# One transfer instead of two for each of Q, K and V of a batch

## The chip, the cores and the metric

The kernel runs on one core of a Trainium2 chip. The metric is the device time of one execution in microseconds (us), less is better. The engines have short names: PE multiplies matrices (PEld is its weight load), DVE and ACT work on vectors, POOL and SP issue transfers here. Sixteen DMA engines move data between the chip's main memory and the core's on-chip memory, which has 128 partitions.

## What is computed

A sliding-window attention over 8 batches, 8 heads, 576 positions and 64 columns feeds a mixture of experts with 32 slots. Heads 0 to 3 are *plain*: a query sees the last 32 positions. Heads 4 to 7 are *dilated*: it sees every fourth of the last 128.

```python
batch, n_heads, seq, head_dim = (8, 8, 576, 64)

scores = scale * np.matmul(q, k.transpose(0, 1, 3, 2))
rel = pos[:, None] - pos[None, :]
mask_plain = (rel >= 0) & (rel < window)
mask_dil = (rel >= 0) & (rel < window * dilation) & (rel % dilation == 0)
masks = np.stack([mask_plain if h < H // 2 else mask_dil for h in range(H)], axis=0)
scores = np.where(masks[None, :, :, :], scores, -1000000000.0)
...
attn = np.exp(scores)
attn = attn / (np.sum(attn, axis=-1, keepdims=True) + 1e-09)
return np.matmul(attn, v).astype(np.float32)
```

The result, turned so that a row holds the 512 columns of one position (8 heads of 64), is the `x` (4608 x 512) of the second part:

```python
logits = x @ phi
d = np.exp(logits - logits.max(0, keepdims=True))
d /= d.sum(0, keepdims=True) + 1e-09
slot_input = (d.T @ x).reshape(E, S_per_e, D)
for e in range(E):
    h = np.maximum(slot_input[e] @ w1[e], 0.0)
    slot_out[e] = h @ w2[e]
c = np.exp(logits - logits.max(1, keepdims=True))
c /= c.sum(1, keepdims=True) + 1e-09
return (c @ slot_out).astype(np.float32)
```

There are 8 experts with 4 slots each; `w1[e]` is 512 x 1024 and `w2[e]` 1024 x 512. All inputs and the output are fp32.

## The kernel before

**Loads.** Every input is fp32 in main memory and is written as fp16 by the transfer itself. All these transfers are issued by POOL (`nc.gpsimd.dma_start`) and run in one queue, in the order of issue; only the constants come from SP. `load_raw(which, b)` brings Q, K or V of batch `b` into a tile of 128 partitions with `PJ * D` = 36 x 64 = 2,304 elements each. A head has 576 positions, that is `PB` = 16 pieces of 36 positions; a piece is one partition's row. Before, the loop over `g` at L188 issues two transfers of 64 rows each: `g = 0` the four plain heads into the even partitions (`t[0::2, :]`), `g = 1` the four dilated heads into the odd ones. Partition 2i holds row i of the plain heads, partition 2i + 1 row i of the dilated ones. Each tile name has two buffers (`bufs=2` of `raw_pool`, L161).

The experts' weights come by `load_w1` (L195, one transfer of 1 MB as written) and `load_w2` (L203, the whole of an expert in 1 MB, for experts 0 to 4; L209, in four transfers of 256 KB each, for experts 5 to 7).

**Turning.** DVE's `turn` (L220) transposes blocks of 32 x 32 words of a raw tile, all 128 partitions at once, in two halves along the row: `QT0`, `QT1` and so on. It puts Q and K into `qT` and `kT` and V into `vT`, in the tiles named `qk` and `vT` by the profile. Plain and dilated rows come out side by side, since their partitions alternate.

**The loop.** The list `ORDER` holds the steps of an iteration with a stage each; a step of stage s works on batch `it - s` (L529 to L537). After the later half of a turn has run, its raw tile is free and the load of the same tensor two batches on is issued (`frees`, `loads`). After V of batch 3 and of each later one a weight is issued too (`load_weights(1)`), and after V of batch 7 all that are left of w1 of the eight experts and w2 of experts 0 to 2. The remaining w2 take the place of the raw tiles and the `qk` tiles; they are issued when the last batch's turns and its scores `S2` are done (L538 to L549).

One iteration works on several batches: scores on PE (L262), exp on ACT (L271), masks on DVE (L282), the product with V on PE (L305), its normalisation (L317, L326, L330), the logits and the sums for the slots (`U`). After the loop PE multiplies the slots by w1 (L598) and w2 (L629), and the result is spread, multiplied by `ET` (L656), scaled (L665, L669) and written out batch by batch (L676, L703), also from POOL's queue.

**Before the loop** (L449 to L465) POOL issues in this order: Q and K of batch 0, V of batch 0, Q and K of batch 1, `phi`, V of batch 1.

Of the kernel before, what the change touches and what calls it, by code (L numbers as in the profile page):

```python
# [31 lines left out]
PJ = S // PB  # L32
# [64 lines left out]
def kernel(  # L97
# [10 lines left out]
    nc = tc.nc  # L108
# [75 lines left out]
    def load_raw(which, b):  # L184
        t = raw_pool.tile([128, PJ * D], FP16, name=f"raw{which}_{b}", tag=f"raw{which}")
        raw[(which, b)] = t
        src = {"Q": q, "K": k, "V": v}[which][b]
        for g in range(2):  # L188
            nc.gpsimd.dma_start(  # L189
                out=t[g::2, :],  # L190
                in_=src[4 * g : 4 * g + 4].rearrange("h (p j) d -> (h p) (j d)", j=PJ),
            )

    def load_w1(e):
        nc.gpsimd.dma_start(  # L195
# [253 lines left out]
    for which in "QK":  # L449
        load_raw(which, 0)  # L450
# [3 lines left out]
    for i in range(2):  # L454
        nc.vector.memset(vX[i][:, :, :, D : D + 1], 1.0)
        for x in (xp_t[i], xd_t[i]):
            nc.vector.memset(x[:, :, 4 * D : 4 * D + 1], 1.0)
    load_raw("V", 0)
    for which in "QK":
        load_raw(which, 1)  # L460
    nc.gpsimd.dma_start(
        out=phi_raw.rearrange("p (u c) s -> p u (c s)", u=2),
        in_=moe_phi.rearrange("(u p c) s -> p u (c s)", u=2, c=2),
# [65 lines left out]
    for it in range(B + max(s for _, s in STEPS)):  # L529
# [20 lines left out]
        if it == 0:  # L550
            nc.vector.tensor_copy(
                out=phi4, in_=phi_raw[:, :, None, :].broadcast_to([128, 4, 4, N_SLOTS])
# [54 lines left out]
    for c in range(8):  # L607
# [3 lines left out]
        out=hTm[:, 0].rearrange("p c (j s) -> p c j s", j=4)[:, :, :, 0:16], in_=hT4[:, :, :, 0:16]  # L611
    )
    nc.scalar.copy(
        out=hTm[:, 1].rearrange("p c (j s) -> p c j s", j=4)[:, :, :, 16:32], in_=hT4[:, :, :, 16:32]
# [87 lines left out]
    for e in range(2):  # L702
        nc.gpsimd.dma_start(  # L703
            out=rest[:, e, 512:576, :].rearrange("n i d -> i n d"), in_=om_l[64 * e : 64 * e + 64]
# [37 lines left out]
```

## Time and profile before

| what | us |
|---|---|
| time, median of 3 runs | 180.59 (180.25 to 180.80) |
| the profiled execution's own time | 180.63 |
| its span | 178.8 |
| busy: PE, DVE, ACT, POOL | 126.7, 126.3, 124.0, 56.2 |
| raw loads: transfers, KB written each, median from issue to landing | 16 each of Q, K and V, 288.0, 9.8 to 10.8 |
| 1 MB weights: transfers, median from issue to landing | 13, 22.1 |

How to read it: the span goes from the first to the last instruction or landing of one profiled execution. "Landing" is the moment when all sixteen DMA engines have signalled that their share of a transfer is written. A transfer waits behind the earlier ones of its queue, so the time from issue to landing is mostly waiting. The page gives the transfers of this execution:

```profile
DMA packets 21445, 40.85 MB, mean 229 GB/s; under 512 B 1712, under 2 KB 14128, under 8 KB 20784
q0 software_dynamic: 21280, 40.41, 114.3%
q1 hardware_dynamic: 144, 0.14, 0.3%
HBM read 62.07 MB, written 9.44 MB: 400 GB/s over the span
```

MB and GB/s in the first three lines count what is written, so an fp32 input counts half of what is read. A packet is one row or piece that a DMA engine moves in one go; the packets under 512 B include each engine's signal at the end of its share of a transfer. Shares over 100% come from packets that overlap on an engine. In lists of instructions a group of the same line is shown with its count (x2), and "L189" is line 189 of the kernel.

### The profile page before, as it was taken

How to read it: one execution, taken by the hardware profiler on the slowest of the kernel's cores; microseconds unless marked ns; L12 is line 12 of the kernel's file. 1: busy time of each engine (PE TensorE's matmuls, PEld its weight loads, DVE VectorE, ACT ScalarE, POOL GpSimd, SP SyncE). 2: the span in 40 equal slices, each digit the busy share in tenths (PEclk: the TensorE clock that was granted, in tenths of full speed). 3: DMA queues.
4: the chain of work that ended last, by engine and by line, in shares of the span. 5: the costliest groups of instructions: out<-in, count | busy, mean ns of one | idle time of the engine just before them, and what ended most of it. 6: DMA issues, size and time to landing. Idle time of an engine off the chain costs nothing.

```text
span 178.8 us, 4810 instructions
## 1 busy us (share of the span) xinstructions
PE 126.7 (71%) x2016; PEld 81.9 (46%) x2016; DVE 126.3 (71%) x277; ACT 124.0 (69%) x268; POOL 56.2 (31%) x94
## 2 busy tenths in 40 slices
PE   0015938988899998888988988986686856688000
PEld 0014625776666676567667657665332422221000
DVE  6464899999999999999999898275211016789200
ACT  6006758999999999999999989996301116688000
POOL 7544244224224224225420005111111515375400
PEclk9999999999999879999999699699957685555555
DMA  5999999999999999999999999999999999999994
GB/s 98 195 208 211 211 213 211 212 213 215 215 213 213 213 213 214 213 211 218 210 213 214 214 215 221 215 218 218 209 211 194 196 197 234 390 321 393 406 413 125
DMA packets 21445, 40.85 MB, mean 229 GB/s; under 512 B 1712, under 2 KB 14128, under 8 KB 20784
## 3 DMA queue, kind: packets, MB, share of 16 engines
q0 software_dynamic: 21280, 40.41, 114.3%
q8 instruction: 16, 0.26, 0.5%
q1 hardware_dynamic: 144, 0.14, 0.3%
q14 instruction: 5, 0.04, 0.1%
HBM read 62.07 MB, written 9.44 MB: 400 GB/s over the span
## 4 chain that ended last, share of the span: by engine, by line
DMA 56%; DVE 25%; PE 5%; issue 4%; ACT 3%; POOL 1%; POOLq 0%; DVEq 0%
DMA w<-in_moe_w_dram 36%; DMA rawK<-in_k_dram 9%; DVE qk L220 8%; DMA rawV<-in_v_dram 5%; DMA phi_raw<-in_moe_phi_dram 5%; DVE vT L220 5%; DVE p L282 5%; PE f L656 3%; ACT om L665 2%; DVE xd L330 2%; DVE om_l L669 1%; DVE xp L330 1%; POOL rawQ L189 1%; PE s L262 1%; DVE rc_P L317 1%
## 5 line engine op out<-in xcount | busy, mean ns | idle before, releaser
L271 ACT ACTIVATE p<-s 128x1920 f16<-128x1920 f32 (+1 forms) x24 | 42.7, 1779 | 10.9 <-PE s L262 10.8
L262 PE MATMUL s<-qk 32*128 32x128 f16 (+2 forms) x704 | 26.7, 295 | 17.9 <-DVE qk L220 12.6
L305 PEld LDWEIGHTS <-p 128*128 128x128 f16 (+1 forms) x480 | 23.0, 105 | 14.7 <-DVE xp L330 5.2
L242 ACT COPY vX<-rv 128x768 f16<-128x768 f16 (+1 forms) x32 | 25.9, 866 | 1.7 <-PE rv L236 1.7
L262 PEld LDWEIGHTS <-qk 32*128 32x128 f16 x704 | 17.2, 117 | 21.1 <-DVE qk L220 12.6
L326 ACT ACTIVATE xp<-o_P,rc_P 128x64 f16<-128x64 f32 x96 | 24.3, 406 | 2.7 <-DVE rc_P L317 2.7
L282 DVE TENSOR_TENSOR p<-p,masks 128x1920 f16<-128x1920 f16 (+1 forms) x24 | 25.4, 1083 | 0.0
L236 PE MATMUL rv<-cst,vT 128*128 128x128 f16 x176 | 18.7, 252 | 3.5 <-DVE vT L220 1.8
L220 DVE STREAM_TRANSPOSE qk<-rawQ 128x576 uint32<-128x576 uint32 x16 | 18.8, 1242 | 2.7 <-DMA rawQ<-in_q_dram 2.7
L305 PE MATMUL o_P<-vX,p 128*128 128x65 f16 (+1 forms) x288 | 20.0, 205 | 0.8 <-DVE xd L330 0.2
L220 DVE STREAM_TRANSPOSE qk<-rawK 128x576 uint32<-128x576 uint32 x16 | 19.5, 1231 | 1.1 <-DMA rawK<-in_k_dram 1.1
L220 DVE STREAM_TRANSPOSE vT<-rawV 128x576 uint32<-128x576 uint32 x16 | 19.5, 1226 | 0.7 <-DMA rawV<-in_v_dram 0.4
L236 PEld LDWEIGHTS <-vT 128*128 128x128 f16 x176 | 13.8, 128 | 8.2 <-issue 3.7
L209 POOL DMA_DIRECT2D w<-in_moe_w_dram x12 | 8.9, 746 | 26.7 <-DMA w<-in_moe_w_dram 18.7
L669 DVE TENSOR_SCALAR om<-f,rrow 128x256 f16<-128x256 f32 (+1 forms) x28 | 13.5, 519 | 4.1 <-PE f L656 3.4
L189 POOL DMA_DIRECT2D rawQ<-in_q_dram x16 | 8.9, 560 | 21.0 <-DVE rc_P L317 16.0
L665 ACT ACTIVATE om<-f,rrow 128x256 f16<-128x256 f32 (+1 forms) x28 | 12.8, 502 | 3.5 <-PE f L656 2.8
L656 PE MATMUL f<-so_sb,ET 32*128 32x256 f16 (+1 forms) x60 | 12.1, 420 | 3.7 <-ACT om L665 2.5
L676 POOL DMA_DIRECT2D out_dram<-om x14 | 10.4, 745 | 12.4 <-DVE om L669 9.4
L189 POOL DMA_DIRECT2D rawK<-in_k_dram x16 | 8.8, 551 | 17.4 <-DVE rc_P L317 15.0
L305 PE MATMUL o_D<-vX,p 128*128 128x65 f16 x128 | 10.1, 206 | 3.3 <-DVE xp L330 2.8
L189 POOL DMA_DIRECT2D rawV<-in_v_dram x16 | 8.7, 548 | 11.3 <-DVE rc_P L317 8.5
(83 smaller groups left out, 194.3 us busy)
## 6 DMA issues: line engine op xcount, KB each, us to landing
w<-in_moe_w_dram POOLq DMA_DIRECT2D x13, 1024.0 KB, 22.1
out_dram<-om POOLq DMA_DIRECT2D x12, 512.0 KB, 6.2
rawQ<-in_q_dram POOLq DMA_DIRECT2D x16, 288.0 KB, 10.8
rawK<-in_k_dram POOLq DMA_DIRECT2D x16, 288.0 KB, 10.1
rawV<-in_v_dram POOLq DMA_DIRECT2D x16, 288.0 KB, 9.8
w<-in_moe_w_dram POOLq DMA_DIRECT2D x12, 256.0 KB, 15.8
out_dram<-om POOLq DMA_DIRECT2D x2, 1024.0 KB, 8.7
out_dram<-om_l POOLq DMA_DIRECT2D x2, 512.0 KB, 9.3
```

Source lines behind the costliest of these rows:

```text
L189: nc.gpsimd.dma_start(out=t[g::2, :], in_=src[4 * g : 4 * g + 4].rearrange("h (p j) d -> (h p) (j d)", j=PJ),)
L220: nc.vector.transpose(out=out_, in_=in_)
L236: nc.tensor.transpose(rg[:, n_t, :, c, :], rows, ident)
L242: copy(out=vX[b % 2][:, t0 : t0 + n, :, 0:D], in_=rg.rearrange("p n h c d -> p n h (c d)"))
L262: nc.tensor.matmul(sps[:, h, c0 : c0 + w], kk, qq, start=(tt == 0), stop=(tt == 1))
L271: return nc.scalar.activation(out=pt, in_=sps[:, :, 0:n], func=AF.Exp, scale=SCALE)
L282: return nc.vector.tensor_tensor(out=pt, in0=pt, in1=m, op=ALU.mult)
L305: nc.tensor.matmul(o[rows, h, :], lhs, rhs, start=(n == 0), stop=(n == len(jobs) - 1), skip_group_check=True,)
L326: nc.scalar.activation(out=dst[:, h], in_=src[:, h], func=AF.Copy, scale=rc[:, h : h + 1])
L656: nc.tensor.matmul(fp[:, 0 : c1 - c0], ET[32 * j : 32 * j + 32, m : m + 128], so_sb[32 * j : 32 * j + 32, c0:c1], start=True, stop=True,)
L665: nc.scalar.activation(out=dst, in_=fp[:, 0 : c1 - c0], func=AF.Copy, scale=rrow[:, blk : blk + 1])
L669: nc.vector.tensor_scalar(out=dst, in0=fp[:, 0 : c1 - c0], scalar1=rrow[:, blk : blk + 1], scalar2=None, op0=ALU.mult)
```

## The change

```diff
@@ -185,11 +185,9 @@
         t = raw_pool.tile([128, PJ * D], FP16, name=f"raw{which}_{b}", tag=f"raw{which}")
         raw[(which, b)] = t
         src = {"Q": q, "K": k, "V": v}[which][b]
-        for g in range(2):
-            nc.gpsimd.dma_start(
-                out=t[g::2, :],
-                in_=src[4 * g : 4 * g + 4].rearrange("h (p j) d -> (h p) (j d)", j=PJ),
-            )
+        nc.gpsimd.dma_start(
+            out=t, in_=src.rearrange("(g h) (p j) d -> (h p) g (j d)", g=2, j=PJ)
+        )
 
     def load_w1(e):
         nc.gpsimd.dma_start(
```

The two transfers of 64 rows become one of 128. Its destination is the whole tile. Its source is walked as 64 rows, and at each row first the plain heads' and then the dilated heads' 2,304 elements, which lie 4 x 576 x 64 elements further on. Each partition receives what it received before. The function is called 24 times, so there are 24 transfers instead of 48. Nothing else is changed.

## The prediction

> **What bounds the kernel now.** I began with the page's summary by slices and its chain of waits. In the first fence the digits are tenths of each fortieth of the span (4.47 us), the GB/s row is what the DMA engines wrote, and the last two lines are the chain of work that ended last, by engine and by line.
>
> ```profile
> DMA  5999999999999999999999999999999999999994
> GB/s 98 195 208 211 211 213 211 212 213 215 215 213 213 213 213 214 213 211 218 210 213 214 214 215 221 215 218 218 209 211 194 196 197 234 390 321 393 406 413 125
> DMA 56%; DVE 25%; PE 5%; issue 4%; ACT 3%; POOL 1%; POOLq 0%; DVEq 0%
> DMA w<-in_moe_w_dram 36%; DMA rawK<-in_k_dram 9%; DVE qk L220 8%; DMA rawV<-in_v_dram 5%; DMA phi_raw<-in_moe_phi_dram 5%; DVE vT L220 5%; DVE p L282 5%; PE f L656 3%; ACT om L665 2%; DVE xd L330 2%; DVE om_l L669 1%; DVE xp L330 1%; POOL rawQ L189 1%; PE s L262 1%; DVE rc_P L317 1%
> ```
>
> The DMA engines are full in every slice but the first and the last, at about 213 GB/s while fp32 inputs are written as fp16 and at about 400 GB/s while results go out. So I asked whether the queue ever runs dry. POOL issues everything from one queue, so I read its timeline around the loads, and the windows of the middle.
>
> ```profile
> 5.71 0.60 POOL L189 DMA_DIRECT2D rawK<-in_k_dram  x1
> 7.02 0.55 POOL L189 DMA_DIRECT2D rawK<-in_k_dram  x1 [0.71 <-DMA rawQ<-in_q_dram]
> 11.83 0.54 POOL L189 DMA_DIRECT2D rawV<-in_v_dram  x1 [0.84 <-DMA rawV<-in_v_dram]
> 22.64 1.09 POOL L189 DMA_DIRECT2D rawQ<-in_q_dram  x2 [2.54 <-DVE qk L220]
> 47.39 1.09 POOL L189 DMA_DIRECT2D rawQ<-in_q_dram  x2 [4.03 <-DVE rc_P L317]
> 91.46 0.53 POOL L203 DMA_DIRECT2D w<-in_moe_w_dram  x1 [0.83 <-DMA rawV<-in_v_dram]
> 106.95 1.05 POOL L203 DMA_DIRECT2D w<-in_moe_w_dram  x2 [14.96 <-DVE rc_P L317]
> 142.83 0.74 POOL L209 DMA_DIRECT2D w<-in_moe_w_dram  x1 [0.59 <-DMA w<-in_moe_w_dram]
> ```
>
> Start, length, what is issued; in brackets how long POOL stood still first and for whom. Up to 17.4 us, and again from 84 us, POOL waits for landings. The signals of the landings in the trace use eight semaphores in turn, so the ninth transfer is issued when the first has landed. From 20 to 82 us it waits until DVE's turns of a batch (L220) free one of the two buffers. Neither lets the queue run dry. rawQ of batch 5, issued at 47.39, stands behind transfers that land until 57.09; the weight issued at 106.95 stands behind five whole weights and lands at 132.34. The landing signals confirm it: the last of the sixteen engines signals one load of 288 KB after another some 1.39 us apart and one weight of 1 MB some 4.9 us apart, with no hole but single stalls below 1 us, until the last weight at 153.24. After that an output of 512 KB follows every 1.3 us, with two of 2.5 us among them for the outputs of 1 MB, and the last landing is at 177.27. The end is set by the **stream of transfers on its slowest engine**, from its first packet at 2.65 us on. The DVE share of the chain is in the first 54 us, where loads are ready before their use: V of batch 1 landed at 21.49 and its turn began at 25.59; V of batch 4 at 52.19 and 64.70. That pace decides nothing as long as w2 of experts 3 and 4 can be issued before the backlog ends at 127.20; they are issued at 106.95, which is 20 us of slack.
>
> **The change part by part.** (1) *48 loads of 64 rows become 24 of 128.* The bytes stay (24 x 576 KB written), and so does the row that one packet moves: the trace has 3,072 packets of 4,608 B. What goes is 24 transfers' worth of cost per transfer. To price it I took the gap between landings for the first engine to signal, for four kinds of transfer, with the share of one engine in each:
> - raw half: 1.387 us, 4 packets, 36,864 B of source;
> - w1 (L195): 4.896 us, 16 packets, 131,072 B;
> - whole w2 (L203): 4.864 us, 8 packets, 131,072 B;
> - a quarter of w2 (L209): 1.339 us, 32 packets, 32,768 B.
>
> I write each as bytes/r + a per packet + s per transfer. w1 less w2: 8a = 32 ns, a = 4.0 ns. w2 less raw: 94,208 B/r = 4,864 - 1,387 - 16 = 3,461 ns, r = 27.2 B/ns. Then raw gives s = 1,387 - 1,354 - 16 = 17 ns. The quarter of w2, which was not used, would be 1,204 + 128 + 17 = 1,349 against 1,339, so s lies between 7 and 17 by these rows. The completion signals themselves (4 B packets) took 22 ns in the median, a third value. Saved: 24 x 17 ns = **0.41 us**, bounds 24 x 7 = 0.17 and 24 x 22 = 0.53. I take 17, since it comes from the very transfers that change.
>
> The Trainium skill, in "DMA: Bandwidth & Descriptors", section "Anatomy of one DMA", says the semaphore write at a transfer's end costs about one cycle and is essentially free on trn2. By that the sum would lose its only gain and the kernel would stay at its time; the trace's 22 ns for such a packet and the 17 ns above speak for a little more, though not for more than the measurement can tell.
>
> (2) *The first load.* Data of the first half begins at 2.65 us, 0.73 us after its issue (1.26 to 1.92) ends. The load of 128 rows has one issue, and its source has a further dimension (the pair of heads). What does that cost?
>
> ```profile
> L189 POOL DMA_DIRECT2D rawQ<-in_q_dram x16: 542/548/662, 1.3 to 74.0; - x16
> L203 POOL DMA_DIRECT2D w<-in_moe_w_dram x5: 528/536/558, 88.3 to 107.5; - x5
> L195 POOL DMA_DIRECT2D w<-in_moe_w_dram x8: 713/728/741, 29.5 to 86.9; - x8
> L703 POOL DMA_DIRECT2D out_dram<-om_l x2 | 1.3, 636 | 0.6 <-issue 0.6
> ```
>
> The first three give shortest, median and longest issue in ns, the last the mean behind the bar. 64 rows cost 548 ns and 128 rows 536 ns (L203), so the number of rows costs nothing; a further dimension costs 636 (L703, 64 partitions with four pieces each) to 728 ns (L195). So an issue lasts 0.54 to 0.73 us, and the first, 0.66 now, between 0.66 and 0.85. I add **0.10 us** to the start of the stream, by L703, the nearest; bounds 0 and 0.66, the latter if the first issue does take the time of two.
>
> (3) *POOL's other 24 issues* fall away: 24 x 0.55 = 13.2 us of POOL's 56.2, less 24 x 0.09 for the further dimension. I count them at nothing, because POOL's waits hide them: 94.1 us of waiting before the issues at L189, L203 and L209 (49.7 + 17.7 + 26.7). Without that cover one load's issue, 0.55 us against 1.39 us of moving, would still not starve the queue. Phi, the weights and every later load stand behind fewer issues and in the same order.
>
> (4) *The eight semaphores* are used up half as fast by loads. K of batch 1 is issued about 4 us instead of 5.71 and 7.02, phi and V of batch 1 right behind, so POOL runs further ahead until the two buffers stop it, with Q of batch 3 (22.64 now) at the latest. An earlier place in a queue that is never empty is worth nothing. If the queue did run short somewhere, this would be a gain, at most the 0.66 us in the first rival below.
>
> (5) *DVE's turns* need both halves now, so they wait for the same last byte. No wait is added.
>
> Sum: -0.41 + 0.10 = -0.31 us. From the profiled execution's 180.63 us (span 178.8 and 1.8 around it; it is 0.04 above the median of 180.59) this gives **180.3 us**, 0.2% less. I take 0.3%, 0.54 us, as what a measurement of this kernel can tell from no change, so the forecast is *no change that can be told*; by the bounds of its terms 180.1 to 181.1.
>
> **The rivals.**
> *A larger gain: the stall in the start goes too.* The third load landed 2.05 us after the second instead of 1.39; six or seven packets around 5.95 to 6.2 us took 0.5 to 1.45 us instead of 0.36. That is while POOL still issues and only halves are queued. With whole loads 0.66 us would go besides: 180.63 - 0.31 - 0.66 = 179.7. For it: it fell in the stretch with the most issues. Against it: seven transfers were already in the queue. The floor is a raw load without any cost beside its bytes: 48 x (1,387 - 1,354) = 1.6 us, 179.0.
>
> *Slower: two places in the source.* A half reads one run of 64 rows; the merged load goes back and forth between row i and row i + 64, 589,824 B further on. If a packet that starts elsewhere costs x more, the price is 24 x 8 x = 192x on each engine, and from x = 4.4 ns on (0.54 + 0.31 = 0.85 us over 192) it is slower. Bounds for x: w1's source goes back and forth too (u in L197, halves 1 MB apart), and its packets carry 4 ns in all, so nearly 0; the first packets of the stream took 494 to 899 ns instead of 361, so hundreds where a place is cold. At 8 ns it would be 180.63 - 0.31 + 1.54 = 181.9. Against it speaks w1, which is much the nearer.
>
> *No gain at all:* s belongs to packets, or the first issue takes twice as long: 180.63 + 0 to 0.66 - 0 to 0.41, between 180.6 and 180.9.
>
> *The whole fixed time per transfer goes.* The first half took from 1.26 to 5.34, of which 1.39 is its moving, 2.7 us besides; 24 x 2.7 = 65 us would leave 116. The gaps of 1.387 us between landings exclude it as long as the queue is full. The Trainium skill's fit in the same page, section "Anatomy of one DMA", is 2.0 us plus bytes over 436 GB/s for one transfer; by that it would be 24 x 2.0 = 48 us, 133 us, and the trace shows that this part overlaps with the neighbours.
>
> *The change does not do what it says:* the program splits the load again, 48 transfers, 180.6.
>
> **How the numbers follow.** Forecast 0.43, of which 0.09 lies more than 0.54 us below the time before and 0.02 above, since the runs scatter by 0.55 us and the slowest engine's stalls may fall otherwise; larger gain 0.25; slower 0.18; no gain 0.10, of which 0.02 over 0.54 us above; fixed time 0.02; split again 0.02. Faster: 0.25 + 0.02 + 0.09 = 0.36; slower: 0.18 + 0.02 + 0.02 = 0.22; within 0.3%: 0.32 + 0.08 + 0.02 = 0.42. The time is that of the forecast, 180.3. The range of 8 in 10 takes in the larger gain down to its floor, 179.0, and the slower case up to x = 7 ns, 181.6.
>
> **What would show it.** Landing gaps of about 2.75 us per whole load (2 x 1,354 + 32 + 17), 24 such issues of 0.54 to 0.73 us, 3,072 packets of 4,608 B still, and 384 fewer under 512 B than the 1,712 now; first packet at 2.65 to 2.85 us; the last weight at about 152.9. Wrong would be: a landing gap above 2.79 us (two places), a stretch of the middle below 200 GB/s, another lag between the first and the last engine than now (1.0 us at 12 us, 3.2 us at 150), or a first load that lands after 6.9 us.

## The result and the profile after

The changed kernel takes 179.31 us (median of 6 runs, 179.04 to 179.51) against 180.51 us before (6 runs, 180.25 to 180.80): a ratio of 0.9932, 95% interval 0.9919 to 0.9945. That is 1.2 us or 0.7% less, more than the 0.3% taken above as what can be told from no change. The profiled execution has 179.36 us, its span 177.5.

First the rows of the page after that answer to those shown of before: DMA by slices, the transfers, and the chain that ended last, by engine and by line.

```profile
DMA  5999999999999999999999999999999999999995
GB/s 90 211 214 211 214 212 215 215 213 217 214 213 216 212 215 212 212 216 216 216 211 215 214 215 223 211 220 220 209 216 190 196 197 224 387 347 394 405 414 142
DMA packets 21061, 40.85 MB, mean 230 GB/s; under 512 B 1328, under 2 KB 13744, under 8 KB 20400
DMA 46%; ACT 23%; DVE 9%; PE 9%; POOL 4%; issue 3%; POOLq 0%; DVEq 0%; ACTq 0%
DMA w<-in_moe_w_dram 38%; DMA phi_raw<-in_moe_phi_dram 8%; ACT p L269 5%; ACT vX L240 5%; ACT xp L324 4%; PE f L654 3%; DVE qk L218 3%; DVE vT L218 3%; ACT om L663 2%; ACT xT L363 2%; PE rv L234 2%; ACT xT L365 2%; POOL w L193 2%; PE s L260 2%; ACT xd L324 1%
```

The engines are as full as before and the bytes are the same. 384 small packets are gone (1,712 less 1,328): sixteen signals for each of 24 transfers. The second slice, about 4.4 to 8.9 us, carries 211 GB/s where it had 195. The chain is led through other engines in the middle (ACT where DVE stood), which work beside the stream in both kernels; its last part is the same, the weights with 38% and then the outputs. The next fence has POOL's timeline after (start, length, what, and in brackets the idle time ahead and its cause) and, in its last line, the shortest, median and longest issue in ns.

```profile
1.27 0.69 POOL L188 DMA_DIRECT2D rawQ<-in_q_dram  x1 [0.82 <-POOLq L724]
9.51 0.59 POOL L188 DMA_DIRECT2D rawQ<-in_q_dram  x1 [3.71 <-DVE qk L218]
22.03 0.59 POOL L188 DMA_DIRECT2D rawQ<-in_q_dram  x1 [6.40 <-DVE qk L218]
L188 POOL DMA_DIRECT2D rawQ<-in_q_dram x8: 588/593/819, 1.3 to 72.3; - x8
```

POOL no longer waits for landings in the start: from 9.51 us on only a buffer holds it. The queue was never short of work either way, so this by itself shows no gain. To see where time went, the windows of the start are read at both kernels. Columns: the window, its length, busy us of PE, PEld, DVE, ACT and POOL (with counts), granted clock, DMA share, GB/s. Before:

```profile
2.50:5.00 2.50, 0.00 (x0) 0.00 (x0) 1.44 (x3) 1.45 (x6) 2.50 (x5) 1.00 0.99 162
5.00:9.00 4.00, 0.00 (x0) 0.00 (x0) 2.17 (x2) 0.00 (x0) 1.86 (x4) 1.00 1.03 192
12.00:24.00 12.00, 7.79 (x126) 5.76 (x126) 8.20 (x9) 7.67 (x7) 4.71 (x9) 1.00 1.08 212
```

After:

```profile
2.50:5.00 2.50, 0.00 (x0) 0.00 (x0) 1.44 (x3) 1.45 (x6) 2.50 (x6) 1.00 0.96 146
5.00:9.00 4.00, 0.00 (x0) 0.00 (x0) 2.13 (x2) 0.00 (x0) 0.80 (x2) 1.00 1.06 214
12.00:24.00 12.00, 7.78 (x126) 5.78 (x126) 8.22 (x9) 7.67 (x7) 1.78 (x3) 1.00 1.08 213
```

Between 5 and 9 us the engines move 214 GB/s instead of 192, after a slower first 2.5 us; in a second execution of each kernel it is 215 instead of 199. From 12 us on there is hardly a difference to be seen in GB/s. The signals of the landings are finer. For two profiled executions of each kernel (us; the last of the sixteen engines to signal, unless said otherwise):

| | before | before, second | after | after, second |
|---|---|---|---|---|
| V of batch 0 landed | 12.93 | 12.60 | 12.38 | 12.29 |
| lag of the last engine behind the first there | 1.04 | 0.76 | 0.47 | 0.39 |
| from there to the last weight | 140.31 | 140.40 | 139.78 | 139.86 |
| the same, first engine to signal | 138.14 | 138.14 | 137.67 | 137.79 |
| from the last weight to the end | 24.02 | 24.03 | 23.87 | 23.87 |
| the end | 177.27 | 177.02 | 176.03 | 176.03 |

So of the 1.12 us between the means of the ends, 0.43 come in the first 12 us, 0.53 over the 21 loads after V of batch 0 and the weights, and 0.16 at the outputs.

### The profile page after: what moved, and what is told of

Its sections match the earlier page's. It is cut to its first block, busy times and chain, and to the rows that moved or that the text cites. A ratio compares the mean times of both kernels' runs of the same rounds, so it can differ in the third digit from the quotient of the medians.

```text
span 177.5 us, 4765 instructions
## 1 busy us (share of the span) xinstructions
PE 122.4 (69%) x2016; PEld 79.8 (45%) x2016; DVE 126.3 (71%) x277; ACT 123.8 (70%) x268; POOL 44.5 (25%) x70
## 2 busy tenths in 40 slices
DMA packets 21061, 40.85 MB, mean 230 GB/s; under 512 B 1328, under 2 KB 13744, under 8 KB 20400
## 4 chain that ended last, share of the span: by engine, by line
DMA 46%; ACT 23%; DVE 9%; PE 9%; POOL 4%; issue 3%; POOLq 0%; DVEq 0%; ACTq 0%
DMA w<-in_moe_w_dram 38%; DMA phi_raw<-in_moe_phi_dram 8%; ACT p L269 5%; ACT vX L240 5%; ACT xp L324 4%; PE f L654 3%; DVE qk L218 3%; DVE vT L218 3%; ACT om L663 2%; ACT xT L363 2%; PE rv L234 2%; ACT xT L365 2%; POOL w L193 2%; PE s L260 2%; ACT xd L324 1%
## 5 line engine op out<-in xcount | busy, mean ns | idle before, releaser
L269 ACT ACTIVATE p<-s 128x1920 f16<-128x1920 f32 (+1 forms) x24 | 44.5, 1854 | 10.3 <-PE s L260 10.2
L240 ACT COPY vX<-rv 128x768 f16<-128x768 f16 (+1 forms) x32 | 27.7, 944 | 1.7 <-PE rv L234 1.7
L324 ACT ACTIVATE xp<-o_P,rc_P 128x64 f16<-128x64 f32 x96 | 26.7, 503 | 2.5 <-DVE rc_P L315 2.5
L303 PEld LDWEIGHTS <-p 128*128 128x128 f16 (+1 forms) x480 | 22.4, 103 | 13.4 <-issue 3.9
L234 PE MATMUL rv<-cst,vT 128*128 128x128 f16 x176 | 18.2, 250 | 3.1 <-DVE vT L218 1.8
L188 POOL DMA_DIRECT2D rawQ<-in_q_dram x8 | 5.1, 633 | 29.5 <-DVE rc_P L315 18.6
L363 ACT COPY xT<-rp 128x576 f16<-128x576 f16 x16 | 11.3, 876 | 1.1 <-PE rp L344 1.1
L365 ACT COPY xT<-rd 128x576 f16<-128x576 f16 x16 | 10.6, 787 | 0.0
```

The lines of the kernel that those rows point to most:

```text
L234: nc.tensor.transpose(rg[:, n_t, :, c, :], rows, ident)
L240: copy(out=vX[b % 2][:, t0 : t0 + n, :, 0:D], in_=rg.rearrange("p n h c d -> p n h (c d)"))
L269: return nc.scalar.activation(out=pt, in_=sps[:, :, 0:n], func=AF.Exp, scale=SCALE)
L303: nc.tensor.matmul(o[rows, h, :], lhs, rhs, start=(n == 0), stop=(n == len(jobs) - 1), skip_group_check=True,)
L324: nc.scalar.activation(out=dst[:, h], in_=src[:, h], func=AF.Copy, scale=rc[:, h : h + 1])
L363: copy(out=xT_t[b][:, c, :], in_=rg[:, 0:S])
```

## The experiments

Ratios are to the kernel before, measured beside each, with 95% intervals.

**e1, which loads give the gain: the first six.** The six loads ahead of the loop are whole, the others halves.

```diff
     def load_raw(which, b):
...
+        if b < 2:
+            nc.gpsimd.dma_start(
+                out=t, in_=src.rearrange("(g h) (p j) d -> (h p) g (j d)", g=2, j=PJ)
+            )
+            return
         for g in range(2):
```

> Only the six loads of batches 0 and 1 (those issued before the loop) are whole transfers; the other eighteen loads stay two halves. Theory A (a completion cost of about 22 ns per transfer, and besides it a stall of some 0.6 us at the start that only halves have): 0.13 + 0.55 less than before, about 179.8 us, and the lag between the first and the last engine to signal at 12 us is about 0.5 us, not 1.0. Rival B (all of the gain is a cost per transfer, 1.2 us over 24, 50 ns each): 180.2 us. Rival C (the stall at the start is chance and belongs to no form of the load): 180.4 us and a lag at 12 us of either size.

Measured: 179.72 us against 180.79, ratio 0.9947 (0.9931 to 0.9962), 1.0 us less; the lag at 12 us is 0.40. The interval of the gain is 0.7 to 1.2 us: Theory A's 0.7 is its lower end, and Rival B's 0.3 is too little. In the trace the end comes 0.74 us earlier than in the two of before (mean).

**e2, the other eighteen.** The same with `if b >= 2`.

> The complement: batches 0 and 1 in halves as before, the eighteen later loads whole. Theory A: 18 x 22 ns = 0.4 us less than before, about 180.1 us, a lag of about 1.0 us between first and last engine at 12 us as before, and landing gaps of 2.75 us for the whole loads. Rival B (50 ns per transfer): 179.6 us. Rival C: 180.1 us, with a lag of either size.

Measured: 180.23 against 180.79, ratio 0.9977 (0.9961 to 0.9993), 0.4 us less; the lag at 12 us is 1.47. That is Theory A's number; the 0.9 us of Rival B lies outside the interval, 0.1 to 0.7 us. On the first engine whole loads in a row landed about 2.75 us apart. The gains of the two experiments, 1.0 and 0.4, add up to the 1.2 of the change within their intervals.

**e3, halves cut the other way.** Two transfers again, but each takes plain and dilated rows in turn.

```diff
-        for g in range(2):
-            nc.gpsimd.dma_start(
-                out=t[g::2, :],
-                in_=src[4 * g : 4 * g + 4].rearrange("h (p j) d -> (h p) (j d)", j=PJ),
-            )
+        rows = src.rearrange("(g h) (p j) d -> (h p) g (j d)", g=2, j=PJ)
+        for m in range(2):
+            nc.gpsimd.dma_start(out=t[64 * m : 64 * m + 64, :], in_=rows[32 * m : 32 * m + 32])
```

> All loads are two transfers again, but cut across partitions 0 to 63 and 64 to 127 instead of even and odd ones: each takes 32 rows of the plain and 32 of the dilated heads in turn, as the whole load does. Theory A: the count of transfers is that of before, so the completion cost stays: 180.5 us if the stall at the start belongs to halves, 180.0 if it belongs to a first touch of one region after another. Rival D (the gain comes from the order of the source or from whole runs of partitions, not from the count): 179.3 us.

Measured: 180.13 against 180.79, ratio 0.9977 (0.9962 to 0.9991), 0.4 us less, nearer to the second number of Theory A than to the first and far from Rival D. The window from 5 to 9 us, with as many transfers as before, lies between those of the two kernels:

```profile
5.00:9.00 4.00, 0.00 (x0) 0.00 (x0) 1.83 (x2) 0.00 (x0) 1.90 (x5) 1.00 1.03 207
```

So part of the gain is not the count of transfers but the order in which the source is read; or the run of partitions that is written, which changed with it. In the trace little of it lies at the start: V of batch 0 landed at 12.64 us, where the two traces of before have 12.93 and 12.60. From there to the last weight the last engine took 139.96 us instead of 140.31 and 140.40, the first one 138.11, as before.

**e5 and e6, source or destination.** The two crosses: `out=t[64 * g : 64 * g + 64, :]` with the source of before, and `out=t[m::2, :]` with the source of the last experiment.

> Two halves per load with the source of before (one group of heads after the other), but written to partitions 0 to 63 and 64 to 127 instead of even and odd ones, so rows come to other partitions than the computation wants; all instructions and bytes are those of before. If the stall in the first 9 us comes from the source's order (one group of heads, all sixteen engines in one region of 590 KB): late packets in the load of K of batch 0 as before (3 to 5 us over all engines), a lag of 1.0 us or more at 12 us, about 180.5 us. If it comes from the destination's step of two partitions: none there, a lag of about 0.8 us, about 180.1 us.

> The other cross: two halves per load, each with 32 rows of the plain and 32 of the dilated heads in turn, but written to even and to odd partitions, so again rows come to other partitions than the computation wants. If the source's order makes the stall: no late packets after the first load, a lag of about 0.8 us, about 180.1 us. If the step of two partitions makes it: late packets in K of batch 0, a lag of 1.0 us or more, about 180.5 us.

Measured: the first 180.35 against 180.38, ratio 0.9997 (0.9984 to 1.0010), no difference; the second 180.12 against 180.38, ratio 0.9988 (0.9975 to 1.0002), which by itself can't be told from none. Window from 5 to 9 us of the first (one group of heads after the other, neighbouring partitions):

```profile
5.00:9.00 4.00, 0.00 (x0) 0.00 (x0) 2.20 (x2) 0.00 (x0) 1.60 (x4) 1.00 1.04 203
```

and of the second (both groups in turn, even and odd partitions):

```profile
5.00:9.00 4.00, 0.00 (x0) 0.00 (x0) 2.01 (x2) 0.00 (x0) 2.15 (x5) 1.00 1.07 213
```

These two windows by themselves decide nothing: in the 2.5 us ahead of them the first ran at 168 GB/s and the second at 136, so from 2.5 to 9 us they moved about the same, 1.23 and 1.19 MB. The packets tell more. The first has late packets in K of batch 0, though 1.2 us of them where 3 to 5 were expected, and a lag of 1.29; the second has one late packet, of 0.6 us, where none was expected, and a lag of 0.82.

**before_again and after_again, is the stall chance?** Both kernels once more, for a second trace.

> The kernel before once more, for a second trace. If the stall at the start belongs to the form of its loads: late packets in K of batch 0 again (more than 1 us over all engines), lag at 12 us 1.0 us or more. If it is chance: it may be gone.

> The changed kernel once more, for a second trace. If the absence of the stall belongs to the form of its loads: under 0.3 us of late packets in K of batch 0, lag at 12 us about 0.5 us. If it is chance: it may be there.

Measured: 180.38 and 179.36 us; the lag at 12 us was 0.76 before, less than expected, and 0.39 after. What is seen in all traces of halves and whole loads together, as the time that the packets of K of batch 0 took beyond their usual 361 ns, added up over the engines, and the lag at V of batch 0:

| the first loads | traces | late packets of K, us | lag, us |
|---|---|---|---|
| halves, one group of heads each | before twice, e2, e5 | 3.2, 1.8, 4.9, 1.2 | 1.04, 0.76, 1.47, 1.29 |
| halves, both groups in turn | e3, e6 | 0.0, 0.6 | 0.78, 0.82 |
| whole | after twice, e1, e7 | 0.0, 0.0, 0.0, 0.0 | 0.47, 0.39, 0.40, 0.62 |

(e7, told below, has the first loads of the changed kernel.) Among the halves, late packets of K come with one group of heads at a time, wherever it is written, and with both in turn they are nearly gone; 1.2 against 0.6 us is a narrow gap, though, with two traces on one side. What the order of the source is worth in time is not shown: V of batch 0 landed at 12.60 to 13.45 us with one group of heads and at 12.63 and 12.64 with both. Only the whole loads stand clear of all halves, in the lag and in the landing of V, at 12.27 to 12.45 us. With both groups in turn the lag does not come from K: it is 0.77 (e3) and 0.64 us (e6) at the end of Q already. Why sixteen engines that read one group serve some packets late just at the second tensor, and not later in the run, stays open.

**e4 and e8, more transfers.** Four of 32 rows per load, 96 in all, first with the groups of heads apart:

```diff
         for g in range(2):
-            nc.gpsimd.dma_start(
-                out=t[g::2, :],
-                in_=src[4 * g : 4 * g + 4].rearrange("h (p j) d -> (h p) (j d)", j=PJ),
-            )
+            for m in range(2):
+                h0 = 4 * g + 2 * m
+                nc.gpsimd.dma_start(
+                    out=t[64 * m + g : 64 * m + 64 : 2, :],
+                    in_=src[h0 : h0 + 2].rearrange("h (p j) d -> (h p) (j d)", j=PJ),
+                )
```

> Four transfers of 32 rows per load, 96 in all, 48 more than before. Theory A: 48 x 22 ns = 1.05 us more, about 181.6 us, with landing gaps of about 0.70 us (2 x 339 + 2 x 4 + 22 ns), and perhaps 0.5 us more of stalls at the start. Rival B (50 ns): 182.9 us. If POOL's issues (0.55 us each) or the eight semaphores starve the queue, more than 183 us, with a DMA share under 1.0 in some window of the middle.

Measured: 184.20 against 180.79, ratio 1.0190 (1.0162 to 1.0219): 3.4 us more, far over Theory A. Quarters in a row land 0.705 us apart, two of them 1.41 against 1.387 for a half, which is the 22 ns expected and gives 1.1 us. The other 2.3 us lie in stretches, as windows of that kernel show:

```profile
2.00:12.00 10.00, 0.00 (x0) 0.00 (x0) 5.29 (x6) 1.47 (x7) 7.62 (x16) 1.00 0.99 179
12.00:22.00 10.00, 6.34 (x110) 4.75 (x111) 6.11 (x8) 5.52 (x5) 7.69 (x16) 1.00 1.09 207
22.00:32.00 10.00, 6.19 (x112) 4.45 (x110) 9.69 (x18) 6.71 (x13) 6.44 (x13) 1.00 1.05 201
40.00:64.00 24.00, 20.64 (x413) 15.00 (x406) 22.96 (x50) 23.42 (x51) 10.79 (x21) 0.93 1.06 212
64.00:72.00 8.00, 6.56 (x143) 4.87 (x140) 7.46 (x16) 7.45 (x17) 3.69 (x8) 0.79 1.04 197
72.00:82.00 10.00, 8.14 (x138) 6.04 (x137) 9.51 (x23) 9.47 (x21) 5.48 (x11) 0.94 1.01 186
```

In the slow windows, under 205 GB/s, packets of many loads are late. They are not simply those in which POOL issues most: from 12 to 22 us it is busy for 7.69 of 10 us and the engines move 207 GB/s, from 64 to 72 us for 3.69 of 8 and they move 197. A DMA share under 1.0, which was expected if the queue starved, shows at the start alone (0.99). One line of POOL's timeline:

```profile
74.39 0.50 POOL L191 DMA_DIRECT2D rawK<-in_k_dram  x1 [5.42 <-DMA w<-in_moe_w_dram]
```

K's last quarter waits 5.42 us for a weight, since the landings use eight semaphores in turn, so that eight transfers are under way at most, and now a quarter of 144 KB uses up one of the eight places.

Then the same count with both groups in turn (`rows[16 * m : 16 * m + 16]` to `t[32 * m : 32 * m + 32]`, m from 0 to 3):

> Four transfers per load as in the quarters of 32 rows that took 3.4 us more than before, but each takes 16 rows of the plain and 16 of the dilated heads in turn and goes to 32 neighbouring partitions; the result is the reference's. If those 3.4 us came from the number of transfers (eight in flight, POOL's dense issues): about 184 us again, with windows below 200 GB/s in the middle. If more than 2 us of them came from reading one group of heads at a time: about 181.3 us (48 x 20 ns = 1.0 more than before, less 0.3 at the start), over 208 GB/s in every window after 20 us.

Measured: 183.23 against 180.52, ratio 1.0163 (1.0124 to 1.0202), 2.7 us more. That is nearer to the count's number than to the order's, although no window of the middle falls below 200 GB/s in this trace. The windows of its profiled execution, which was its quickest at 182.61 us, are low mainly in the start:

```profile
2.00:12.00 10.00, 0.00 (x0) 0.00 (x0) 5.08 (x6) 1.49 (x7) 7.39 (x15) 1.00 0.97 177
22.00:32.00 10.00, 6.20 (x112) 4.47 (x110) 9.70 (x17) 6.50 (x13) 6.88 (x15) 1.00 1.05 205
72.00:82.00 10.00, 8.09 (x141) 5.82 (x140) 9.64 (x23) 9.47 (x21) 6.68 (x13) 1.00 1.05 210
```

So reading both groups in turn does not save transfers of 32 rows: late packets of K are there again, 4.6 us of them. From 72 to 82 us POOL is busier than in the first kernel of quarters (6.68 us instead of 5.48) and yet the engines move 210 GB/s instead of 186, so POOL's issuing alone does not make a window slow. Small transfers cost more than their signals, and this part was not traced to its cause: the eight places, POOL's issues beside the running transfers, or the few rows per engine.

**e7, a step further.** The changed kernel with the quarters of w2 (L209 before) joined to halves, so 6 transfers instead of 12:

```diff
-        for u in range(2):
-            nc.gpsimd.dma_start(out=w2t[e][:, 4 * u : 4 * u + 4, cols], in_=src[:, 4 * u : 4 * u + 4, cols])
+        nc.gpsimd.dma_start(out=w2t[e][:, :, cols], in_=src[:, :, cols])
```

> The changed kernel with each pair of quarters of w2 of experts 5 to 7 in one transfer too: 6 instead of 12, the same packets of 512 B, six transfers fewer in all. By the completion cost of about 20 ns per transfer: 0.12 us less than the changed kernel, about 179.2 us against a before of about 180.5. By rival B (50 ns): 0.3 us less. If the end of the input stream becomes coarser for the multiplications with w2 (the first of them starts when 512 KB have landed instead of 256), up to 0.2 us more.

Measured: 179.19 against 180.52, ratio 0.9924 (0.9908 to 0.9940). It is the lowest median, but its interval and that of the changed kernel, 0.9919 to 0.9945, overlap almost wholly, so no further gain is shown; 0.1 us could not have been seen.

## Why the prediction was right or wrong

*What bounds it: right.* The end follows the stream of transfers on its last engine. The end moved by 1.12 us in the traces (means of two) and the time by 1.2; DVE, ACT and PE have the work of before.

*Cost per transfer: right.* The first engine's time from V of batch 0 to the last weight shrank by 0.41 us (means of two) with 21 transfers fewer: 19 ns each, where the sum had 17 and the bounds 7 to 22. Whole loads in a row land 2.74 and 2.76 us apart (medians of the two traces), as forecast. The eighteen later loads alone (e2) shortened that stretch by 0.23 us, 13 ns each, and the time by 0.4 us with an interval of 0.1 to 0.7, which fits all of these prices. The Trainium skill's rule ("DMA: Bandwidth & Descriptors", "Anatomy of one DMA"), that the signal at the end is almost free, is neither confirmed nor refuted: 13 to 19 ns per transfer are measured, and no run shows how much of it is the signal itself.

*Which engine the price was taken from: incomplete.* I priced the gap between landings on the first engine to signal, while the text had the end set by the slowest. On that one the same stretch shrank by 0.53 us. The 0.12 us more are no price of a transfer: in e3, with no transfer fewer, the last engine's stretch is 0.4 us shorter too. The lag between the engines is what the sum had no term for. It was on the list of signs of being wrong, as 1.0 us at 12 us and 3.2 at 150, and it came out otherwise: 0.47 and 0.39 us at 12 us, and 2.58 and 2.46 at the last weight.

*The first load: the step that failed.* "I add 0.10 us to the start of the stream." The first issue took 0.69 us (0.66 to 0.85 forecast), other issues 0.59 in the median, as the bounds had it. The term itself came out smaller: the first packet began 0.03 and 0.02 us later than in the two traces of before, and Q landed at 6.84 and 6.72 us instead of 6.73 and 6.78. But V of batch 0 landed 0.43 us *earlier* on the last engine (means of two), where the stall at K did not come and the lag was smaller at Q already. I had it as a rival with a chance of 0.25, at 179.7 us, and set the chance low because seven transfers were already in the queue. That argument answers a queue that runs dry, and the packets were late in a queue that was full. The whole loads at the start alone (e1) gave 1.0 us, most of the gain. The forecast of no change was thus the wrong case, and the measured time lies 0.4 us below the right rival's, within the range. That the range holds it is owed to this rival and its floor; the sum alone was off by 1.0 us.

*The rival of two places in the source: not borne out.* It had reading two regions in turn cost time. At the start it is one region at a time that has the late packets, while two in turn have few or none at halves (e3, e6). In the middle a gap of 2.74 to 2.76 us, with about 2.75 forecast, leaves no price for it.

*The eight places* ("worth nothing"): right for 48 and for 24 transfers. At 96 they are seen in POOL's waits.

*The fixed time per transfer* and *the split again* are excluded by 1.2 us and by 384 signals fewer. Another sentence of the same page of the Trainium skill fits: its section "Rules for kernel authors" advises one transfer of 128 partitions in place of two to disjoint halves, since both use the same engines. The two halves of e3 and the whole load differ by 0.8 us in favour of the whole (0.9977 against 0.9932, each against before).

The outputs' 0.16 us between the last weight and the end were not forecast. In the traces this stretch is 23.87 to 23.93 us where the first loads are whole (after, e1, e7) and 23.99 to 24.09 where they are halves; why is open.

## What to carry to other kernels

Where one queue is full from start to end, ask besides the price of a transfer how far the last engine lags behind the first, and where that lag arises: here a lag from the start was still there at the last weight. In the ten traces with halves or whole loads it grew by 1.85 to 2.27 us between V of batch 0 and the last weight, whether it began at 0.39 or at 1.47. A join of transfers that saves 13 to 19 ns each, 0.3 to 0.5 us in all, gained 1.2 us, because it also changed how the first loads land. Splitting is not the mirror image: 48 more transfers cost 2.7 to 3.4 us here where 24 fewer gained 1.2.

## What was not expected of the hardware

All sixteen engines in one region of 590 KB at the start served 5 to 12 packets of the second tensor more than 0.1 us late, by up to 0.9 us each (four traces). In the six traces in which each transfer took two regions in turn and 64 rows or more there was one such packet; with 32 rows (e4, e8) there were 13 and 12. Issues of whole loads followed each other 0.52 to 0.70 us apart at the start, while each is shown with 0.64 to 1.12 us, so in the trace POOL's issues overlap there.
